# Attention and expert layer on one core: all four value products of a unit in one slot, sums and gates' products behind them

## The chip, the core and the metric

The kernel runs on one core of a Trainium2 chip. The core has TensorE (PE), VectorE (DVE), ScalarE (ACT), GpSimd (POOL) and SyncE (SP, which here only issues DMAs). The metric is the device time of one execution in microseconds, as the median of several runs. The inputs are fixed: 8 batches, 12 heads, 448 tokens, head size 64 in float32, and an expert layer over 3584 tokens with 8 experts.

## The reference, cut to what matters

```python
def rmsnorm(x, g):
    rms = np.sqrt(np.mean(x * x, axis=-1, keepdims=True) + 1e-06)
    return x / rms * g
q_n, k_n = rmsnorm(q, g_q), rmsnorm(k, g_k)
scores = np.matmul(q_n, k_n.transpose(0, 1, 3, 2)) / np.sqrt(64)
scores = scores - np.max(scores, axis=-1, keepdims=True)
attn = np.exp(scores)
attn = attn / (np.sum(attn, axis=-1, keepdims=True) + 1e-09)
x = np.matmul(attn, v)                      # -> 3584 x 768, heads next to each other
logits = x @ w_gate + modality_bias[modality_id]
# the expert with the largest logit takes the token:
#   out = probability * (relu(x @ w1[e]) @ w2[e])
```

## The kernel before, in words

The attention is cut into 48 units (`NU`) of two heads. A unit has 7 slots (`NJ`), one for each chunk of 128 of its 896 keys (the middle chunk has an end of each head). The program is written out slot by slot by the loop over `n`. What a slot does stands in a table, `plan`, which is filled from the dictionary `PLAN`: `put(slot, name, unit)`. Unit `u` has its exponentials in slots 7u to 7u+6; its other steps lie slots earlier or later. Every engine works off its own instructions strictly in the order in which they were written, so a step that waits holds all that is behind it on its engine. In one slot PE gets, in this order: the score products of the chunk (`st`), the products for the maxima of a unit two units ahead (`sa`), value products (`av`), sums (`sums`), gates' products (`gates`), transposes of keys or queries (`tr`), of the maxima (`mt`), of sums and gates (`recips`), of the output (`xt`).

The steps that the change and the prediction name, with the slot within a unit (0 to 6) before the change:

- `st`, line 849: two products (four in slot 3) into one of two PSUM banks; ACT takes the exponential out of it into `p`.
- `sa`, line 821 (816 in slot 3): one product into one of two PSUM banks (`ps_a`); DVE reduces it to the maximum of each query (`at_hlw<-sa`). The `sa` of a slot needs the bank that the reduction two slots before has read.
- `tr`, line 750: four transposes of the keys in slot 0 and of the queries in slot 3, into one of the two PSUM banks of `ps_t`, which `mt`, `recips` and `xt` share in rotation. Their operands are split into a high and a low part. ACT copies the high part (`xw<-tr`, next slot), DVE subtracts it from the value (`xw<-tr`), and DMAs that SP issues (line 763, `w1w<-xw`) move halves to the other 64 partitions. ACT makes two more copies, the last in the slot after the next. The queries' transposes are in slot 3, and the first `sa` that reads their moved half is in slot 0 of the next unit, four slots later.
- `mt`, line 832: slot 1; a transpose of the maxima, an ACT copy, and a DMA (line 837) that carries them as one more row to the score products, six slots later.
- `av`, line 888: the value products of the unit before, a pair (one for each head) for each of four chunk positions. Pairs 0, 1 and 2 are 128 rows by 64 columns, pair 3 is 64 rows by 64 columns, both heads at once in different columns of the array. Each product appears as two records of PE. Before: pairs 0 and 1 in slot 1, pair 2 in slot 4, pair 3 in slot 6. ACT copies the finished values out in the slot after pair 3 (`avcopy`).
- `sums`, line 903: every second unit, in slot 2; four products with 32 columns each that add up the exponentials over the partitions. Their operands are partial sums over the chunks (`csum`: one operation on DVE, `r2w<-r2w,half`, the others on POOL).
- `gates`, line 910: every fourth unit, in slot 6; four products with 32 columns each.
- `recips`, line 922: every fourth unit, in slot 2, three slots after the gates' products; transposes, and on DVE the reciprocals of the sums and the gate logits.
- `xt`, line 945: slot 4; four transposes of a unit's values, which DVE scales by the reciprocals (`at_w2hb<-xt,rs` or `yw<-xt,rs`); after every third unit SP issues a DMA of the rows to memory (line 961).

DVE also has the sums of squares of queries and keys (`at_hlw<-xrw`, after an ACT square), and many small operations: the inverse roots (`rstd`) and the routing (`route`, `route_pos`, `tables`). These small operations are taken from a queue by `pump`, so many a slot: nine a unit by the numbers in `pmpa` and `pmp`, most of them in slots 2 to 6. POOL multiplies the normalised queries and keys, adds partial sums, and issues the gathers and scatters.

After the attention come the experts: slots of 256 tokens with products against `w1` (line 480) and `w2` (line 510). The last units' ends are written out among the first of these.

Of the kernel before, what the change touches and what calls it, by code (L numbers as in the profile page):

```python
# [17 lines left out]
B, H, S, D = 8, 12, 448, 64  # L18
NT, DM, DFF, NE = 3584, 768, 1024, 8
CP, NCH = 112, 4  # L20
NJ = 7
NP = H // 2
NU = B * NP
# [8 lines left out]
ET = mybir.EngineType  # L32
PLAN = {'rtj': 6, 'rushat': 36, 'av': (1, 1, 4, 6), 'xt': 4, 'xte': (2, 5), 'sm': 2, 'la': 6, 'rc': 9, 'csv': (1,), 'csj': (3, 6), 'csd': (1, 1), 'cse': (2, 1), 'sa': 14, 'mt': 6, 'tk': 21, 'tq': 18, 'nq': 26, 'nk': 26, 'sk': 49, 'sq': 50, 'rs': 48, 'ld': 58, 'first': {('sq', 0): -22, ('sk', 0): -22, ('nk', 0): -21, ('nq', 0): -20, ('sq', 1): -21, ('sk', 1): -21, ('sq', 2): -20, ('sk', 2): -20, ('nk', 1): -18, ('nq', 1): -18, ('tk', 0): -18, ('tq', 0): -18, ('sa', 0): -14, ('tk', 1): -13, ('tq', 1): -11, ('sa', 1): -7, ('mt', 0): -6, ('tk', 2): -8, ('tq', 2): -8, ('nq', 2): -14, ('nk', 2): -14, ('nq', 3): -2, ('nk', 3): -1, ('sq', 3): -8, ('sk', 3): -8, ('sq', 4): -9, ('sk', 4): -9, ('sq', 6): -6, ('sk', 6): -4, ('sk', 7): -7, ('sq', 8): 5, ('sk', 8): 5, ('nk', 7): 15, ('nq', 9): 31, ('tq', 3): 4, ('mt', 1): 0, ('nq', 5): 10, ('mt', 8): 50, ('rs', 0): -21, ('rs', 2): -18, ('nq', 8): 35, ('rs', 5): -7, ('mt', 2): 8, ('nq', 7): 18, ('mt', 5): 30, ('sk', 9): 15, ('tk', 9): 43, ('mt', 6): 36, ('nq', 6): 13, ('sa', 5): 22, ('rs', 7): 0, ('rs', 8): 6, ('mt', 4): 22, ('nk', 4): 4, ('ld', 9): 6, ('tk', 5): 15}, 'rs0': {0: 0, 2: 1, 5: 0, 7: 0, 8: 2}, 'sastep': 1, 'start': -22, 'warm': {5: 2, -6: 16, -12: 4, -7: 2, -9: 4, -21: 4}, 'warmn': 2, 'early': 1, 'late0': 1, 'pmp0': 2, 'ramp': 10, 'pmp': (0, 0, 1, 1, 1, 0, 1), 'nv': [(2, 1)], 'pmpa': (1, 0, 1, 0, 1, 1, 1), 'rush': (1, 1, 1), 'ps': [(7, 1)], 'pa': [(6, 0), (6, 1), (5, 1), (5, 0)], 'rtr': 6, 'sml': 4}
MANUAL = {ET.PE, ET.DVE, ET.Activation, ET.Pool, ET.SP}
# [3 lines left out]
class Deferred:  # L38
    """Engine calls go out at once, or into the open queue."""

# [16 lines left out]
def deferred(fn):  # L57
    """What fn issues, as queue items."""
    Deferred.queue = items = []
    fn()  # L60
    Deferred.queue = None
    return items
# [3 lines left out]
def kernel(  # L66
# [25 lines left out]

    # ---------------------------------------------------------------- constants
    idn = cp.tile([128, 128], F32, name="idn")
# [83 lines left out]

    # ---------------------------------------------------------------- slot tables
    def prefix(src, nm, n):  # L180
# [19 lines left out]
    def tables(nm, ns, cnt, nb, taken, e_prev, half_blocks=None):  # L200
# [7 lines left out]
        if taken is not None:  # L208
            # blocks of at most half the size go last: columns of their own
            br = slice(NE, nv)  # L210
            nb_e = nb
            nb, cnt_e, cnt = tl("nb", [128, nv]), cnt, tl("cnt", [128, nv])
            V.scalar_tensor_tensor(out=nb[:, br], in0=nb_e, scalar=2.0, in1=half_blocks, op0=ALU.mult,
                                   op1=ALU.subtract)
            V.tensor_tensor(out=nb[:, ar], in0=nb_e, in1=nb[:, br], op=ALU.subtract)
            V.tensor_tensor(out=nb[:, ar], in0=nb[:, ar], in1=taken, op=ALU.subtract)
            for c in (ar, br):
                V.tensor_copy(out=cnt[:, c], in_=cnt_e)
# [44 lines left out]
        if taken is not None:  # L263
            # tokens of the slot
            rem = tl("rem", [128, ns], I32)
            V.tensor_tensor(out=rem, in0=cs, in1=js, op=ALU.subtract)
# [24 lines left out]
    def lists(nm, s0, ns, tb, two):  # L291
# [16 lines left out]
        def fin(a, n):  # L308
# [263 lines left out]
    def small_slot(s, xr):  # L572
        """A slot of at most 32 tokens, in a quarter of the array's columns: four column blocks at once."""
        tb, i_ = tb_of(s)
# [64 lines left out]

    # ---------------------------------------------------------------- attention  # L640
    if True:
# [100 lines left out]
        def tr(u, g):  # L742
            t, nm = T[u], "qk"[g]
            ps = ps_t.tile([128, 512], F32, tag="t", name=f"tr{u}_{g}")
            src = t["n" + nm].rearrange("p c h d -> p c (h d)")
            # keys in their own order, queries by chunk of the load
            sp = ps[:, :S].rearrange("p (t c) -> p c t", c=NCH) if g else \
# [53 lines left out]

        # Both heads' tokens on one axis, cut in chunks of 128: the middle one has an end of each.
        def columns(t, j):
            """Head and columns of the chunk's tokens."""
            if j == 3:
# [51 lines left out]
        def csum(u, h):  # L857
# [4 lines left out]
            c2 = c2_b[:, h]  # L862
            # the middle chunk's rows of this head, and the first of its chunks
            if h in CSV:
# [30 lines left out]

        # Four units at a time, each in its 32 columns of the array: the gate's products of both
        # heads in rows 0 to 15, the sums of the exponentials in rows 16 and 17.
        def sums(u):
# [151 lines left out]
        last, lastput = [-99], [-99]  # L1050
        # slots between what gives the operands and the call
        gap = {"op": 0, "act": 3, "pe": 3}
# [43 lines left out]
        for u in range(3, 6):  # L1096
            load(u)
        # engine calls of the slots to come, before and after the slot's exponential
        pre = {e: {} for e in "AV"}
# [18 lines left out]

        # what each slot does; the first units follow each other more closely
        plan = {}  # L1120

        def put(n, *what):
            plan.setdefault(n, []).append(what)
# [14 lines left out]
        for u in range(NU):  # L1138
# [4 lines left out]
            if u < NU - 1:  # L1143
                for c in range(4):
                    put(NJ * (u + 1) + (AVJ[c] if u < NU - 2 else min(AVJ[c], 6)), "av", u, c)
            put(xt_at(u), "xt", u)
            if u % 2:
                put(NJ * (u + 1) + (SMJ if u < NP * (B - 2) else P["sml"]), "sums", u - 1)
            if u % 4 == 3:
                put(NJ * (u + 2) + (LAJ if u < NP * (B - 2) else min(LAJ, 4)), "gates", u // 4)  # L1150
                put(NJ * (u + 2) + (RCJ if u < NP * (B - 2) else min(RCJ, 6)), "recips", u // 4)
            put(when("tk", u), "tr", u, 1)
# [12 lines left out]
        for n in range(P["start"], NJ * NU):  # L1165
# [100 lines left out]
            if (i + 1) % 3 == 0 and 0 < (i + 1) // 3 < 2 * B:  # L1266
                load_v((i + 1) // 3)
        # the last units' ends, among the first slot's products
        after = []

        def go(*fs):
            """Issue the calls; what a call returns (evacuations) goes out after the next one."""
            for f in fs:
# [44 lines left out]

        # the slots: the next one's operands are made among the products of this one
        small = []  # L1320
# [5 lines left out]
        for s in range(NSTAT):  # L1326
            # calls after the products of a beat
            beat = {}
# [113 lines left out]
```

## Time and profile before

| | |
|---|---|
| median of 3 runs | 1171.19 us (1169.7, 1171.19, 1174.05) |
| span of the profiled execution | 1169.2 us, 19997 instructions |
| PE / PE weight loads busy | 1105.2 us (95%) / 865.2 us (74%) |
| DVE / ACT / POOL busy | 954.4 (82%) / 815.7 (70%) / 635.6 us (54%) |
| mean granted clock of TensorE | 0.969 |
| first and last `mt` | 33.2 and 605.4 us |

The profiled execution has no other time of its own than its span. The attention's units run from about 33 to 620 us. In the views an instruction is shown by its start, its length (or, in groups, busy time and mean length), its engine, the line of the program, and output and inputs by the program's names. Most lines of DVE, ACT and POOL read L51 or L52, a helper, so these are told apart by their tiles. Matmuls are pipelined: the distance between the starts of two neighbours says more than the length of one. "<-" behind a wait names what ended it. The granted clock is a share of full speed.

### The profile page before, as it was taken

What the parts mean: (1) busy time and instruction counts of PE and PEld (TensorE: products, weight loads), DVE (VectorE), ACT (ScalarE), POOL (GpSimd) and SP (SyncE); (2) the same over time, 40 slices, a digit from 0 to 9 for tenths busy, and PEclk for the clock granted to TensorE, in tenths of its full rate; (3) what the DMA queues carried; (4) which work ended last, traced back from release to release, by engine and by line L of the source; (5) the groups of instructions that cost most, each with busy time, mean ns of one, the idle gap of its engine ahead of it and who ended that gap; (6) DMA issues with size and microseconds to landing.
All of it is one profiled execution on the core that took longest, in us unless ns stands there. A gap on an engine that the chain in (4) does not pass through costs nothing.

```text
span 1169.2 us, 19997 instructions
## 1 busy us (share of the span) xinstructions
PE 1105.2 (95%) x6678; PEld 865.2 (74%) x6678; DVE 954.4 (82%) x1812; ACT 815.7 (70%) x1569; POOL 635.6 (54%) x575
## 2 busy tenths in 40 slices
PE   8899999999989999898899999999999999999993
PEld 6555665655556555455457898999999999999991
DVE  6987889999999999899978996778677777767770
ACT  6677878777767777575566764787666877667770
POOL 3467666777567775566665456533344324454340
PEclk8899999999999999898899999999999999999997
DMA  7655557666566665454354121111153111111260
GB/s 186 148 134 144 146 152 180 166 161 153 139 141 166 164 156 142 121 138 105 102 176 157 63 42 55 52 32 54 29 217 108 42 55 42 28 55 55 69 217 17
DMA packets 101345, 131.78 MB, mean 113 GB/s; under 512 B 29979, under 2 KB 95983, under 8 KB 99696
## 3 DMA queue, kind: packets, MB, share of 16 engines
q1 hardware_dynamic: 83588, 88.57, 30.2%
q0 software_dynamic: 17616, 41.80, 11.2%
q8 instruction: 57, 0.93, 0.4%
q14 instruction: 56, 0.46, 0.2%
q10 hardware_dynamic: 28, 0.01, 0.0%
HBM read 148.74 MB, written 22.38 MB: 146 GB/s over the span
## 4 chain that ended last, share of the span: by engine, by line
PE 65%; DVE 19%; DMA 6%; ACT 4%; issue 2%; POOL 1%; SPq 1%; ACTq 0%; DVEq 0%
PE ph L480 17%; PE py L510 16%; PE st L849 10%; PE av L888 9%; DVE at_hlw L51 4%; PE sa L821 4%; DMA lt<-l_d,tb_li 3%; DVE at_hlw L52 3%; DVE w1w L51 3%; DVE xw L51 2%; PE tr L750 2%; PE px L463 2%; PE xt L945 2%; DMA w1w<-xw 1%; PE sm L903 1%
## 5 line engine op out<-in xcount | busy, mean ns | idle before, releaser
L480 PE MATMUL ph<-xw,w1w 128*128 128x256 f32 x2016 | 247.5, 284 | 3.0 <-DVE hlw L51 2.3
L480 PEld LDWEIGHTS ph<-xw,w1w 128*128 128x128 f32 x2016 | 245.3, 193 | 5.1 <-DVE hlw L51 2.5
L51 DVE TENSOR_TENSOR w1w<-r,w1w 128x256 fp32r<-128x256 f32 x360 | 220.8, 671 | 14.1 <-ACT w1w L51 14.0
L51 ACT CAST w1w<-r 128x256 fp32r<-128x256 f32 x360 | 224.9, 726 | 0.0
L51 DVE TENSOR_REDUCE at_hlw<-sa 128x1 f32<-128x448 f32 x336 | 205.3, 615 | 17.0 <-PE sa L821 11.7
L849 PE MATMUL st<-w1w 128*128 128x448 f32 (+1 forms) x480 | 193.9, 453 | 1.9 <-ACT r2w L51 1.4
L849 PEld LDWEIGHTS st<-w1w 128*128 128x128 f32 (+1 forms) x480 | 108.2, 241 | 45.9 <-ACT r2w L51 19.3
L821 PE MATMUL sa<-w1w 128*128 128x448 f32 (+1 forms) x288 | 114.9, 400 | 22.6 <-DVE at_hlw L51 22.3
L51 POOL TENSOR_TENSOR r2w<-r2w 128x448 f32<-128x448 f32 (+1 forms) x72 | 82.6, 1148 | 81.1 <-DVE r2w L51 33.6
L51 ACT ACTIVATE hhw<-ph 128x512 fp32r<-128x512 f32 x56 | 33.5, 598 | 124.5 <-PE ph L480 124.5
L51 POOL TENSOR_TENSOR xrw<-r,at_hlw 112x512 f32<-112x512 f32 x95 | 97.6, 1048 | 36.9 <-PE tr L750 11.2
L510 PE MATMUL py<-w2lw,hhw 128*128 128x384 f32 x448 | 113.8, 334 | 0.0
L51 ACT ACTIVATE r2w<-st 128x448 f32<-128x448 f32 x168 | 89.3, 541 | 33.3 <-PE st L849 30.4
L849 PE MATMUL st<-w1w,w2ha 65*128 65x448 f32 x288 | 102.4, 376 | 0.0
L51 ACT ACTIVATE at_w2lw<-st 128x448 f32<-128x448 f32 x168 | 87.9, 540 | 12.1 <-PE st L849 10.3
L51 ACT CAST w1w<-tr 64x448 fp32r<-64x448 f32 x96 | 50.5, 526 | 65.3 <-DVE xw L51 64.7
L51 POOL DMA_INDIRECT out_dram<-yw,lb_oi x22 | 26.7, 1214 | 122.2 <-ACT yw L51 112.3
L51 POOL TENSOR_TENSOR r2w<-r2w,at_w2lw 64x448 f32<-64x448 f32 (+1 forms) x48 | 54.8, 1142 | 66.7 <-DVE r2w L51 38.9
L821 PEld LDWEIGHTS sa<-w1w 128*128 128x128 f32 (+1 forms) x288 | 56.9, 198 | 35.2 <-DVE at_hlw L51 32.4
L51 DVE SCALAR_TENSOR_TENSOR hlw<-ph,hhw 128x512 fp32r<-128x512 f32 x56 | 38.7, 691 | 53.2 <-ACT hhw L51 53.2
L510 PEld LDWEIGHTS py<-w2lw,hhw 128*128 128x128 f32 x448 | 80.9, 188 | 0.0
L51 ACT ACTIVATE w1w<-tr,gs 64x448 fp32r<-64x448 f32 x96 | 60.3, 628 | 29.1 <-DVE xw L51 28.4
(296 smaller groups left out, 2414.2 us busy)
## 6 DMA issues: line engine op xcount, KB each, us to landing
w1w<-xw SPq DMA_DIRECT2D x312, 112.0 KB
r<-in_q_dram SPq DMA_DIRECT2D x48, 224.0 KB
r<-in_k_dram SPq DMA_DIRECT2D x48, 224.0 KB
w2ha<-xw SPq DMA_DIRECT2D x72, 112.0 KB
x_d<-at_w2hb SPq DMA_DIRECT2D x8, 672.0 KB
x_d<-yw SPq DMA_DIRECT2D x8, 672.0 KB
r2w<-in_v_dram SPq DMA_DIRECT2D x16, 288.0 KB
at_w2lw<-in_v_dram SPq DMA_DIRECT2D x16, 288.0 KB
```

The source lines that it names most:

```text
L51: return fn(*a, **kw)
L52: Deferred.queue.append((self.kind, lambda: fn(*a, **kw)))
L463: PE.transpose(ps[:, i, 128 * t : 128 * t + 128], xr[t][:, 2 * g + i], idn)
L480: PE.matmul(ps[:, i], lhsT=lt_, rhs=rt_[:, c], start=n == 0, stop=n == 17)
L510: PE.matmul(ps[n][:, :384], lhsT=lt_[:, j, 128 * t : 128 * t + 128], rhs=rt_[:, 384 * n : 384 * n + 384], start=j == 0 and m == 0, stop=j ...
L750: PE.transpose(sp[:, c], src[:, c], idn[:CP, :CP])
L821: PE.matmul(ps[:, :S], lhsT=t["qq"][r, h, a : a + 128], rhs=t["kk"][h][r], start=True, stop=True)
L849: PE.matmul(ps[:, :S], lhsT=l, rhs=t["qq"][:, h] if first else t["ql"][:, h], start=first and (j != 3 or h == 0), stop=not first and (j != ...
L888: PE.matmul(t["av"][64 * h : 64 * h + 64, :S], lhsT=vv[r, u % 3, j], rhs=t["p"][r, j], start=c == 0, stop=c == 3)
L903: PE.matmul(R[g][32 * i : 32 * i + 32, :S], lhsT=sel[:, m], rhs=T[u + i // 2]["cs"][:, i % 2], start=m == 0, stop=False, tile_position=(0, ...
L945: PE.transpose(ps[:CP, 128 * c : 128 * c + 128], T[u]["xt"][:, c * CP : (c + 1) * CP], idn)
```

## The change

All four value pairs of a unit go into slot 1 (`av`). The sums go behind them in slot 1, of the next unit but one instead of the next (`sm`; six slots later than before). The gates' products go behind the sums, into the same slot (`la`, from 6 to 1). The transposes of sums and gates with the reciprocals go from slot 9 (slot 2 of the next unit) to slot 4 (`rc`), and the output transposes from slot 4 to slot 0 of the same unit (`xt`), behind the keys' transposes. The special cases for the last two batches go, since the new slots need none. ACT's copy of the values follows pair 3 and so goes from slot 0 to slot 2. The number of instructions and all other slots stay as they are. The dropped lines that are only comments are left out here.

```diff
-PLAN = {'rtj': 6, 'rushat': 36, 'av': (1, 1, 4, 6), 'xt': 4, 'xte': (2, 5), 'sm': 2, 'la': 6, 'rc': 9, ...
+PLAN = {'rtj': 6, 'rushat': 36, 'av': (1, 1, 1, 1), 'xt': 0, 'xte': (2, 5), 'sm': 1, 'la': 1, 'rc': 4, ...
...
             if u < NU - 1:
                 for c in range(4):
-                    put(NJ * (u + 1) + (AVJ[c] if u < NU - 2 else min(AVJ[c], 6)), "av", u, c)
+                    put(NJ * (u + 1) + AVJ[c], "av", u, c)
             put(xt_at(u), "xt", u)
             if u % 2:
-                put(NJ * (u + 1) + (SMJ if u < NP * (B - 2) else P["sml"]), "sums", u - 1)
+                put(NJ * (u + 2) + SMJ, "sums", u - 1)
             if u % 4 == 3:
-                put(NJ * (u + 2) + (LAJ if u < NP * (B - 2) else min(LAJ, 4)), "gates", u // 4)
-                put(NJ * (u + 2) + (RCJ if u < NP * (B - 2) else min(RCJ, 6)), "recips", u // 4)
+                put(NJ * (u + 2) + LAJ, "gates", u // 4)
+                put(NJ * (u + 2) + RCJ, "recips", u // 4)
```

More of the change, by code (lines that the diff above doesn't have):

```diff
@@ L32 @@
 ET = mybir.EngineType
-PLAN = {'rtj': 6, 'rushat': 36, 'av': (1, 1, 4, 6), 'xt': 4, 'xte': (2, 5), 'sm': 2, 'la': 6, 'rc': 9, 'csv': (1,), 'csj': (3, 6), 'csd': (1, 1), 'cse': (2, 1), 'sa': 14, 'mt': 6, 'tk': 21, 'tq': 18, 'nq': 26, 'nk': 26, 'sk': 49, 'sq': 50, 'rs': 48, 'ld': 58, 'first': {('sq', 0): -22, ('sk', 0): -22, ('nk', 0): -21, ('nq', 0): -20, ('sq', 1): -21, ('sk', 1): -21, ('sq', 2): -20, ('sk', 2): -20, ('nk', 1): -18, ('nq', 1): -18, ('tk', 0): -18, ('tq', 0): -18, ('sa', 0): -14, ('tk', 1): -13, ('tq', 1): -11, ('sa', 1): -7, ('mt', 0): -6, ('tk', 2): -8, ('tq', 2): -8, ('nq', 2): -14, ('nk', 2): -14, ('nq', 3): -2, ('nk', 3): -1, ('sq', 3): -8, ('sk', 3): -8, ('sq', 4): -9, ('sk', 4): -9, ('sq', 6): -6, ('sk', 6): -4, ('sk', 7): -7, ('sq', 8): 5, ('sk', 8): 5, ('nk', 7): 15, ('nq', 9): 31, ('tq', 3): 4, ('mt', 1): 0, ('nq', 5): 10, ('mt', 8): 50, ('rs', 0): -21, ('rs', 2): -18, ('nq', 8): 35, ('rs', 5): -7, ('mt', 2): 8, ('nq', 7): 18, ('mt', 5): 30, ('sk', 9): 15, ('tk', 9): 43, ('mt', 6): 36, ('nq', 6): 13, ('sa', 5): 22, ('rs', 7): 0, ('rs', 8): 6, ('mt', 4): 22, ('nk', 4): 4, ('ld', 9): 6, ('tk', 5): 15}, 'rs0': {0: 0, 2: 1, 5: 0, 7: 0, 8: 2}, 'sastep': 1, 'start': -22, 'warm': {5: 2, -6: 16, -12: 4, -7: 2, -9: 4, -21: 4}, 'warmn': 2, 'early': 1, 'late0': 1, 'pmp0': 2, 'ramp': 10, 'pmp': (0, 0, 1, 1, 1, 0, 1), 'nv': [(2, 1)], 'pmpa': (1, 0, 1, 0, 1, 1, 1), 'rush': (1, 1, 1), 'ps': [(7, 1)], 'pa': [(6, 0), (6, 1), (5, 1), (5, 0)], 'rtr': 6, 'sml': 4}
@@ new lines @@
+PLAN = {'rtj': 6, 'rushat': 36, 'av': (1, 1, 1, 1), 'xt': 0, 'xte': (2, 5), 'sm': 1, 'la': 1, 'rc': 4, 'csv': (1,), 'csj': (3, 6), 'csd': (1, 1), 'cse': (2, 1), 'sa': 14, 'mt': 6, 'tk': 21, 'tq': 18, 'nq': 26, 'nk': 26, 'sk': 49, 'sq': 50, 'rs': 48, 'ld': 58, 'first': {('sq', 0): -22, ('sk', 0): -22, ('nk', 0): -21, ('nq', 0): -20, ('sq', 1): -21, ('sk', 1): -21, ('sq', 2): -20, ('sk', 2): -20, ('nk', 1): -18, ('nq', 1): -18, ('tk', 0): -18, ('tq', 0): -18, ('sa', 0): -14, ('tk', 1): -13, ('tq', 1): -11, ('sa', 1): -7, ('mt', 0): -6, ('tk', 2): -8, ('tq', 2): -8, ('nq', 2): -14, ('nk', 2): -14, ('nq', 3): -2, ('nk', 3): -1, ('sq', 3): -8, ('sk', 3): -8, ('sq', 4): -9, ('sk', 4): -9, ('sq', 6): -6, ('sk', 6): -4, ('sk', 7): -7, ('sq', 8): 5, ('sk', 8): 5, ('nk', 7): 15, ('nq', 9): 31, ('tq', 3): 4, ('mt', 1): 0, ('nq', 5): 10, ('mt', 8): 50, ('rs', 0): -21, ('rs', 2): -18, ('nq', 8): 35, ('rs', 5): -7, ('mt', 2): 8, ('nq', 7): 18, ('mt', 5): 30, ('sk', 9): 15, ('tk', 9): 43, ('mt', 6): 36, ('nq', 6): 13, ('sa', 5): 22, ('rs', 7): 0, ('rs', 8): 6, ('mt', 4): 22, ('nk', 4): 4, ('ld', 9): 6, ('tk', 5): 15}, 'rs0': {0: 0, 2: 1, 5: 0, 7: 0, 8: 2}, 'sastep': 1, 'start': -22, 'warm': {5: 2, -6: 16, -12: 4, -7: 2, -9: 4, -21: 4}, 'warmn': 2, 'early': 1, 'late0': 1, 'pmp0': 2, 'ramp': 10, 'pmp': (0, 0, 1, 1, 1, 0, 1), 'nv': [(2, 1)], 'pmpa': (1, 0, 1, 0, 1, 1, 1), 'rush': (1, 1, 1), 'ps': [(7, 1)], 'pa': [(6, 0), (6, 1), (5, 1), (5, 0)], 'rtr': 6}
```

## The prediction

> **What bounds the kernel now.** I read the page first (span, engines), then the busy time of the engines by stretch, then the waits of TensorE, then one unit of the attention in order of time. The span of the profiled execution is the base of the sum below; the median of the three runs, 1171.19 us, lies 2.0 us above it.
>
> ```profile
> span 1169.2 us, 19997 instructions
> ```
>
> The change acts in the attention alone, so the stretch from 60 to 600 us counts. First fence: all engines by stretch (PE, PEld, DVE, ACT, POOL busy, granted clock, DMA). Second fence: the same stretches for the value products alone (line 888).
>
> ```profile
> 60.00:240.00 180.00, 178.48 (x926) 106.94 (x924) 158.90 (x318) 144.47 (x310) 120.12 (x110) 1.00 0.61 154
> 240.00:420.00 180.00, 171.45 (x876) 101.21 (x876) 171.34 (x331) 131.44 (x287) 125.45 (x116) 0.98 0.63 151
> 420.00:600.00 180.00, 165.32 (x809) 96.69 (x805) 159.75 (x326) 113.32 (x246) 118.46 (x110) 0.93 0.54 141
> ```
>
> ```profile
> 60.00:240.00 180.00, 58.65 (x256) 14.03 (x256) 1.00 0.61 154
> 240.00:420.00 180.00, 55.49 (x238) 13.35 (x240) 0.98 0.63 151
> 420.00:600.00 180.00, 52.08 (x216) 11.90 (x212) 0.93 0.54 141
> ```
>
> A unit has eight value products, and each shows as two PE instructions, so 16 records are a unit. That gives 16.0, 14.9 and 13.5 units, or 11.25, 12.1 and 13.3 us for a unit. In the first third PE is busy 178.5 of 180 us: PE sets the pace, and DVE has 21 us to spare. In the second DVE is busy 171.3 of 180 (11.5 us a unit, 0.58 idle): DVE sets the pace. In the last third neither is full and the granted clock is 0.93. The waits of PE say the same:
>
> ```profile
> PE sa L821 <- DVE at_hlw L51: 22.3, 24, 3.0
> PE st L849 <- DMA w1w<-xw: 0.5, 1, 0.5
> ```
>
> PE waits for DVE's maxima (22.3 us in all), and practically never for the moves of the split operands through SP's queue.
>
> One unit, PE in order of time (start, length, instruction):
>
> ```profile
> 143.75 0.37 PE L821 MATMUL sa<-w1w 128*128 128x448 f32 x1
> ...
> 145.12 1.72 PE L888 MATMUL av<-r2w 128*64 128x448 f32 x8
> 146.78 0.28 PE L832 MATMUL mt<-idn,at_hlw 128*7 128x128 f32 x1
> ...
> 148.61 0.55 PE L750 MATMUL tr<-idn,xrw 112*128 112x112 f32 x4
> 148.92 0.51 PE L849 MATMUL st<-w1w 128*128 128x448 f32 x1
> ...
> 149.48 0.37 PE L821 MATMUL sa<-w1w 128*128 128x448 f32 x1
> 149.78 0.97 PE L888 MATMUL av<-r2w 128*64 128x448 f32 x4
> 150.68 0.65 PE L945 MATMUL xt<-idn,at_w2lw 128*112 128x128 f32 x4
> 151.09 0.51 PE L849 MATMUL st<-w1w 128*128 128x448 f32 x1
> ...
> 151.64 0.37 PE L821 MATMUL sa<-w1w 128*128 128x448 f32 x1
> ...
> 152.26 0.37 PE L821 MATMUL sa<-w1w 128*128 128x448 f32 x1
> 152.56 0.97 PE L888 MATMUL av<-r2w 64*64 64x448 f32 x4
> 153.46 0.56 PE L910 MATMUL sm<-at_w2hb,wg 128*32 128x448 f32 x1
> ...
> 154.34 0.54 PE L849 MATMUL st<-w1w 128*128 128x448 f32 x1
> ...
> 154.93 0.37 PE L821 MATMUL sa<-w1w 128*128 128x448 f32 x1
> ```
>
> Starts are the thing to read. A slot of scores alone, two `st` and one `sa`, takes 0.62 us (151.64 to 152.26), 0.21 a step. A pair of value products costs 0.90 us when it comes alone (149.78 to 150.68); two pairs of the same shape take 1.66 (145.12 to 146.78), so the second costs 0.76. The `sa` ahead of a value run holds PE 0.30 (149.48 to 149.78) where a plain step takes 0.21, and the score pair behind transposes takes 0.55 up to the next `sa` (151.09 to 151.64) where two plain steps take 0.41: 0.09 in, 0.14 out.
>
> **The change, part by part.** Value pairs 2 and 3 (slots 4 and 6) join pairs 0 and 1 in slot 1. Pair 2 has their shape: 0.90 becomes 0.76, and 0.09 + 0.14 of its own slot go, 0.37 in all. Pair 3 has another shape (64 rows): no row shows it behind a 128-row pair. The ends are 0.76 (same shape) and 0.90 (153.46 less 152.56); I take 0.90, since the gates' products behind it, of yet another shape, take 0.88 (to 154.34). It saves its 0.23 of entry and exit. In a sentence apart: the Trainium skill, TensorEngine Tiling (Array Packing), Key Properties, says that a change of tiling mode drains TensorE; by it pair 3 costs the 0.90, without it 0.76, and then PE would save 0.14 more a unit.
>
> The sums come six slots later, behind the values, every second unit:
>
> ```profile
> 158.87 0.57 PE L903 MATMUL sm<-at_w2hb,sel 128*32 128x448 f32 x2
> ...
> 159.76 0.65 PE L922 MATMUL sp<-idn,at_hlw 128*112 128x128 f32 x4
> ```
>
> They keep 0.89 and lose 0.23 of entry and exit: 0.12 a unit. The gates' products, every fourth unit, follow the sums in the same shape: 0.88 to 0.76, 0.03 a unit. The output transposes (0.41) move from slot 4 behind the keys' transposes in slot 0: 0.31 to 0.41, nothing taken. Sum: 0.37 + 0.23 + 0.12 + 0.03 = 0.75 us of PE a unit, 34.5 us over 46 units. That is the ceiling.
>
> Now what is late next. A unit's queries are transposed in slot 3, copied by ACT, and moved to the other partitions by SP; four slots later `sa` of slot 0 reads them.
>
> ```profile
> 161.26 0.55 PE L750 MATMUL tr<-idn,xrw 112*128 112x112 f32 x4
> 161.85 0.53 ACT L51 CAST xw<-tr 128x448 fp32r<-128x448 f32 x1
> 162.41 2.41 SPq L763 DMA_DIRECT2D w1w<-xw  x4
> ...
> 459.03 0.49 SPq L763
> 459.57 2.25 DMA w1w<-xw
> ```
>
> The last two rows are from the chain: one issue 0.49, then 2.25 to landing. Transposes to landing: 1.15 + 0.49 + 0.05 + 2.25 = 3.94 us. Today 6.32 us lie between (148.61 to 154.93), filled by pairs 2 and 3, the output transposes and the gates. After the change only scores are left: 0.31 + 0.76 + 2 x 0.62 + 0.41 = 2.73 us. PE then waits 1.21 us in front of slot 0's `sa`, and everything behind it waits: key transposes, output transposes, the value run. From that `sa` to the queries' transposes it was 4.86 us (143.75 to 148.61); with pair 2 (0.76), pair 3 (0.90) and the output transposes (0.41) it is 6.93, with sums 7.82, with gates too 8.58. Four units: 2 x 6.93 + 7.82 + 8.58 + 4 x 3.94 = 46.0 us, 11.5 each against 11.25: the first third loses 0.25 x 16 = 4.0 us. Ends for the wait: 0 (then 10.4 a unit) and 0.49 more (one other issue ahead in SP's queue).
>
> In the rest DVE decides. The long run of PE delays `sa` of slot 2, and DVE must live on its queue:
>
> ```profile
> L51 DVE TENSOR_REDUCE at_hlw<-sa 128x1 f32<-128x448 f32 x336 | 205.3, 615 | 17.0 <-PE sa L821 11.7 <-PE sa L816 4.5
> L51 DVE TENSOR_REDUCE at_hlw<-xrw 112x8 f32<-112x512 f32 x91 | 61.0, 675 | 6.9 <-ACT xrw L51 6.8
> L51 DVE SCALAR_TENSOR_TENSOR xw<-tr,gs,xw 128x448 fp32r<-128x448 f32 x48 | 32.6, 680 | 19.6 <-ACT xw L51 19.5
> L51 DVE SCALAR_TENSOR_TENSOR r2w<-r2w,half 128x448 f32<-128x448 f32 x24 | 17.7, 736 | 0.0
> L51 DVE TENSOR_TENSOR at_w2hb<-xt,rs 112x512 f32<-112x512 f32 x24 | 16.4, 683 | 5.9 <-PE xt L945 5.8
> L51 ACT ACTIVATE w1w<-tr,gs 64x448 fp32r<-64x448 f32 x96 | 60.3, 628 | 29.1 <-DVE xw L51 28.4
> ```
>
> Two `sa` banks let PE run two slots ahead. Between the maxima of slots 6 and 2 DVE has one sum over keys (0.74), two sums of squares (1.35), two maxima (1.23), the keys' subtraction (0.68) and the moved output scaling (0.68): 4.68, and three of its nine places a unit for small operations at 0.35 (11.5 less 8.4 of large ones, over nine): 5.7 us. PE needs from `sa` of slot 1 to the end of `sa` of slot 2: 0.30 + 3.32 + 0.03 + 0.56 + 0.37 = 4.58, with sums 5.47, with gates 6.2. DVE runs dry only in the last, 0.13 a unit on average. Idle today is 0.58; small operations come unevenly, so I take 0.3, which gains 0.28 a unit over 30 units: 8.4 us. Ends: nothing, and 0.45.
>
> The maxima's transpose (`mt`) follows the run and now takes the PSUM bank of the keys' transposes (two banks in rotation, output transposes between), which ACT frees only with its second copy in slot 2. DVE reaches the subtraction after about 2.7 + 0.35, then two copies of 0.63: 4.3 us against PE's 3.6, so PE waits 0.7 in units without sums. `sa` of slot 2 then ends at 5.3, inside DVE's 5.7: nothing, and 0.7 x 15 = 10 us if DVE's queue is short. ACT's copy of the values moves to slot 2 ahead of the exponential; it lies in that same wait. Reciprocals come five slots earlier; nothing waits for them before slot 0 of the next unit. SP issues the rows of x in slot 1 instead of 5, ahead of the maxima's rows, which have five slots left. POOL's queue keeps its order.
>
> Sum: 1169.2 + 4.0 - 8.4 = 1164.8, as a median 1166.8: I take 1167.
>
> **Rivals.** (B) The moves are no limit (exponentials and maxima pace slots 4 to 6 anyway, or PE is held elsewhere): then the first third gains 0.75 x 16 = 12.0 and with the 8.4 the time is 1151. For it: not one `sa` waits for such a move now. Against: nothing but 2.73 us is left between.
>
> (C) Slower, by the clock. Short stops have already halved it:
>
> ```profile
> 266.18 0.47 PE L821 MATMUL sa<-w1w 128*128 128x448 f32 x1 [1.77 <-DVE at_hlw L51]
> ...
> 265.00:270.00 5.00, 3.82 (x15) 2.51 (x15) 5.00 (x10) 1.41 (x5) 3.78 (x4) 0.78 0.27 62
> 410.00:415.00 5.00, 3.25 (x16) 2.01 (x17) 5.00 (x9) 2.56 (x8) 3.23 (x4) 1.00 0.39 88
> ```
>
> A wait of 1.77 us was followed by 0.78 in its five us; a stretch with PE busy only 3.25 of 5 kept 1.00. After the change every unit has a dense run and then a thin stretch with a 1.2 us wait in it. If the first 360 us fall to the 0.93 of the last third, that costs (0.07 + 0.05) x 180 = 22 us: 1191 less part of the 8.4 already counted, say 1187. It decides from a mean clock of about 0.97 in the first third. The Trainium skill, TensorE: Matmul & The Clock Gate, Why this matters for your kernels, sets the danger at idle gaps over about 3 us; by that this rival would not happen, and the 1.77 us row speaks against the rule.
>
> (D) The packing saves nothing: a pair costs the same wherever it stands, and all else stays: 1171. Against it the 1.66 for two pairs.
>
> **How the numbers follow.** A measurement here tells about 0.5% (6 us) from no change: faster is below 1165, slower above 1177. Forecast 0.42 (its own range 1158 to 1177; it falls below 1165 in 0.18, the same in 0.24), B 0.23, C 0.27, D 0.08 (same 0.05, slower 0.03). Faster 0.41, same 0.29, slower 0.30. The range reaches from B to C: low 1146 (B with DVE's 0.45), high 1190 (C, or 0.49 and the 10 us of `mt` on top of the forecast).
>
> **What would show it.** PE's waits: `sa` for a DMA from `xw`, near 1 us a unit in the first third (B: none). The queries' transposes to the next `sa` of slot 0: 3.9 us, not 5.5 to 6.3. Value run and pair 3 in 3.3 us; if pair 3 takes 0.76, the drain was wrong. First third: still about 16 units in 180 us (B: 17), clock 1.00 (C: below 0.97). `mt` waiting for ACT. I am wrong if the move lands sooner than 2.2 us or if DVE's small operations pile up in slots 2 to 6 while PE stands.

## The result: slower by 7%, and the profile after

| | before | after |
|---|---|---|
| median | 1172.62 us (1169.7 to 1177.33, 4 runs) | 1253.84 us (1253.11 to 1255.52, 4 runs) |
| ratio, 95% interval | | 1.0695 [1.0644, 1.0745] |
| span, mean granted clock | 1169.2 us, 0.969 | 1253.8 us, 0.936 |
| first to last `mt` | 33.2 to 605.4 us | 32.6 to 682.8 us |

The forecast was 1167, in a range up to 1190; the time lies 64 us above that end. The last row of the table places the loss: the attention's units take 650.2 us instead of 572.2, 78.0 of the 84.6 us that the span grew.

The page of the changed kernel, span and engines:

```profile
span 1253.8 us, 19942 instructions
PE 1135.7 (91%) x6678; PEld 900.7 (72%) x6678; DVE 960.1 (77%) x1812; ACT 824.4 (66%) x1569; POOL 635.5 (51%) x575
```

The work is the same (DVE 960.1 us busy against 954.4), and no engine is fuller than before. The same stretches as in the prediction, first all engines (PE, PEld, DVE, ACT, POOL busy, granted clock, DMA), then the value products alone:

```profile
60.00:240.00 180.00, 160.44 (x754) 98.23 (x754) 130.99 (x259) 118.51 (x252) 98.71 (x91) 0.90 0.50 128
240.00:420.00 180.00, 158.04 (x755) 98.14 (x755) 149.59 (x288) 117.88 (x247) 108.87 (x100) 0.90 0.56 134
420.00:600.00 180.00, 158.61 (x766) 100.52 (x764) 152.79 (x297) 117.65 (x250) 109.14 (x101) 0.91 0.53 126
```

```profile
60.00:240.00 180.00, 49.79 (x208) 14.08 (x208) 0.90 0.50 128
240.00:420.00 180.00, 46.99 (x208) 13.45 (x208) 0.90 0.56 134
420.00:600.00 180.00, 44.92 (x198) 13.17 (x200) 0.91 0.53 126
```

At 16 records a unit these are 13.0, 13.0 and 12.4 units: 13.85, 13.85 and 14.5 us each, where it was 11.25, 12.1 and 13.3. PE is busy 160.44 of 180 us where it was 178.48, DVE 130.99 where it was 158.90, and the clock went from 1.00 to 0.90. Over these stretches as a whole nobody is the bound any more; the engines wait for each other. The view of waits (us in all, times, longest) says who:

```profile
DVE at_hlw L51 <- PE sa L821: 90.8, 38, 5.6
ACT w1w L51 <- DVE xw L51: 74.6, 78, 4.8
PE sa L821 <- DVE at_hlw L51: 55.7, 52, 3.0
PE st L849 <- ACT r2w L51: 12.1, 24, 0.9
PE st L849 <- ACT at_w2lw L51: 8.8, 20, 0.9
PE mt L832 <- DVE at_w2hb L51: 0.4, 1, 0.4
PE sa L821 <- DMA w1w<-xw: 0.2, 1, 0.2
```

DVE waits for PE's maxima 90.8 us (11.7 before), and PE waits for DVE's 55.7 us (22.3 before). Both grew: that is no single bound, but two engines that take turns. The two rows of `st` are one wait, for ACT's exponentials, which go into two buffers by turns: 20.9 us (1.4 before). The last row is the one on which the forecast of the first third rested, a `sa` that waits for the move: 0.2 us in the whole run.

One unit, PE in order of time, is the piece to compare with the prediction's:

```profile
151.20 0.37 PE L821 MATMUL sa<-w1w 128*128 128x448 f32 x1
151.50 3.38 PE L888 MATMUL av<-at_w2lw,r2w 128*64 128x448 f32 x16
154.80 0.28 PE L832 MATMUL mt<-idn,at_hlw 128*7 128x128 f32 x1
...
155.38 0.37 PE L821 MATMUL sa<-w1w 128*128 128x448 f32 x1
...
156.62 0.55 PE L750 MATMUL tr<-idn,xrw 112*128 112x112 f32 x4
...
160.33 0.55 PE L849 MATMUL st<-w1w 128*128 128x448 f32 x1 [0.88 <-ACT r2w L51]
...
160.92 0.37 PE L821 MATMUL sa<-w1w 128*128 128x448 f32 x1
...
162.72 3.38 PE L888 MATMUL av<-r2w 128*64 128x448 f32 x16
166.02 0.57 PE L903 MATMUL sm<-at_hhw,sel 128*32 128x448 f32 x2
166.80 0.54 PE L910 MATMUL sm<-at_w2hb,wg 128*32 128x448 f32 x1
167.66 0.28 PE L832 MATMUL mt<-idn,at_hlw 128*7 128x128 f32 x1
```

The run of values takes 3.30 us (151.50 to 154.80); with sums and gates 4.94 (162.72 to 167.66). From the queries' transposes to `sa` of slot 0 it is 4.30 us (156.62 to 160.92), and the row that ends it is not a DMA but `st` waiting for ACT's exponential. This unit is one of the quickest; the median of that stretch is 5.25 us, with a wait for DVE's maxima in it. The same moments with all engines:

```profile
147.95 0.62 DVE L51 TENSOR_REDUCE at_hlw<-sa 128x1 f32<-128x448 f32 x1
...
153.40 0.19 DVE L52 TENSOR_TENSOR at_hlw<-at_hlw 112x48 f32<-112x48 f32 x1
...
155.79 0.62 DVE L51 TENSOR_REDUCE at_hlw<-sa 128x1 f32<-128x448 f32 x1 [2.20 <-PE sa L821]
...
157.20 0.53 ACT L51 CAST xw<-tr 128x448 fp32r<-128x448 f32 x1
157.70 0.54 ACT L51 ACTIVATE r2w<-st 128x448 f32<-128x448 f32 x1
...
157.77 0.62 DVE L51 TENSOR_TENSOR xw<-tr,xw 128x448 fp32r<-128x448 f32 x1 [0.33 <-ACT xw L51]
...
158.43 0.53 ACT L51 CAST w1w<-tr 64x448 fp32r<-64x448 f32 x1 [0.18 <-DVE xw L51]
...
158.86 0.20 ACT L51 CAST w2ha<-tr 64x64 fp32r<-64x64 f32 x1
...
159.07 0.53 ACT L51 CAST w1w<-tr 64x448 fp32r<-64x448 f32 x1
...
159.74 0.98 ACT L51 ACTIVATE r2w<-st 128x448 f32<-128x448 f32 x2
```

Two things are to be seen. DVE stood 2.20 us dry in the run of values: it had finished the maximum of slot 6 at 148.57, ahead of the run, and the last of its queue at 153.59, while the next `sa` (slot 2) came at 155.38. And after the transposes ACT has one queue: copy, exponential, four more copies, and only at 159.74 the exponentials of slots 5 and 6, for which PE's two score banks wait.

Cutting every unit at four instructions gives the ledger on which the rest of this text rests: the start of `sa` in slot 0 (ahead of the keys' transposes), the start of the value run, the start of `mt`, the start of the queries' transposes, and the next `sa` of slot 0. The means of the 35 to 38 units between 100 and 620 us of each kernel, in us:

| kernel | `sa` to run | run to `mt` | `mt` to queries | queries to next `sa` | unit |
|---|---|---|---|---|---|
| before | 1.41 | 1.65 | 2.55 | 6.80 | 12.42 |
| after | 2.54 | 4.24 | 1.85 | 5.40 | 14.03 |
| after, its floor (lowest that recurs, no sums) | 1.80 | 3.30 | 1.82 | 4.30 | 11.22 |
| e1_spread | 1.89 | 2.58 | 1.89 | 6.24 | 12.60 |
| e2_values | 1.58 | 3.57 | 2.40 | 5.54 | 13.09 |
| e4_extra_products | 1.87 | 4.02 | 1.86 | 6.04 | 13.78 |
| e5_small_ops_in_run | 2.09 | 4.05 | 1.82 | 4.90 | 12.87 |
| e8_small_ops_and_products | 1.89 | 3.98 | 1.84 | 5.63 | 13.34 |
| e10_pair2_joined | 1.46 | 2.45 | 2.46 | 6.33 | 12.71 |
| e13_copy_on_dve | 2.30 | 4.14 | 1.82 | 5.05 | 13.32 |

I call the fourth stretch the thin one: after the change PE has only scores there. The three in front of it grew by 3.02 us (5.61 to 8.63); the thin one gave back 1.40.

The waits can be laid on the same stretches, here for 34 of the units after the change and 37 before. After the change PE stands, in gaps of over 0.1 us, for 0.03 us a unit in the three front stretches together, and for 1.58 in the thin one: 1.21 for DVE's maxima, 0.35 for ACT's exponentials (before: 0.46 in the thin one, all for DVE). DVE is busy 95% of the thin stretch, and only 70 and 60% of the two ahead of it. So PE sets the pace of the front, DVE that of the thin stretch. The front is longer than its quickest units for another reason, the clock. The first stretch of two neighbouring units, the unit above and the next:

```profile
148.63:151.50 2.87, 2.87 (x14) 2.35 (x12) 2.87 (x6) 1.93 (x5) 2.00 (x2) 0.59 0.41 135
160.92:162.72 1.80, 1.80 (x14) 1.43 (x12) 1.22 (x2) 1.80 (x4) 1.72 (x2) 1.00 0.82 219
```

PE is busy all the time in both, with 14 records each: 2.87 us at a clock of 0.59, 1.80 at 1.00. Over all these units the granted clock after the change is 0.68, 0.94, 1.00 and 0.95 in the four stretches (before: 0.98, 1.00, 0.99 and 0.95).

### The profile page after: what moved, and what is told of

It reads as the page before. It is cut to its first block, busy times and chain, and to the rows that moved or that the text cites. A ratio compares the mean times of both kernels' runs of the same rounds, so it can differ in the third digit from the quotient of the medians.

```text
span 1253.8 us, 19942 instructions
## 1 busy us (share of the span) xinstructions
PE 1135.7 (91%) x6678; PEld 900.7 (72%) x6678; DVE 960.1 (77%) x1812; ACT 824.4 (66%) x1569; POOL 635.5 (51%) x575
## 4 chain that ended last, share of the span: by engine, by line
PE 61%; DVE 18%; DMA 8%; ACT 6%; issue 4%; POOL 1%; SPq 1%; ACTq 0%; DVEq 0%; POOLq 0%
PE ph L480 16%; PE py L510 15%; PE av L888 11%; PE st L849 8%; DVE at_hlw L51 4%; DVE at_hlw L52 4%; DMA lt<-l_d,tb_li 3%; DMA w1w<-xw 3%; PE sa L821 3%; DVE xw L51 2%; PE tr L750 2%; DVE w1w L51 2%; PE xt L945 2%; PE sm L903 2%; ACT w1w L51 2%
## 5 line engine op out<-in xcount | busy, mean ns | idle before, releaser
L51 DVE TENSOR_REDUCE at_hlw<-sa 128x1 f32<-128x448 f32 x336 | 204.7, 616 | 97.7 <-PE sa L821 90.8
L849 PE MATMUL st<-w1w 128*128 128x448 f32 (+1 forms) x480 | 199.8, 467 | 22.4 <-ACT r2w L51 12.1
L821 PE MATMUL sa<-w1w 128*128 128x448 f32 (+1 forms) x288 | 125.2, 435 | 56.0 <-DVE at_hlw L51 55.7
L849 PEld LDWEIGHTS st<-w1w 128*128 128x128 f32 (+1 forms) x480 | 111.6, 246 | 46.4 <-ACT r2w L51 24.7
L821 PEld LDWEIGHTS sa<-w1w 128*128 128x128 f32 (+1 forms) x288 | 61.0, 212 | 80.7 <-DVE at_hlw L51 76.9
L849 PE MATMUL st<-w1w,w2ha 65*128 65x448 f32 x288 | 106.0, 388 | 0.0
```

What stands on the lines that cost most here:

```text
L51: return fn(*a, **kw)
L821: PE.matmul(ps[:, :S], lhsT=t["qq"][r, h, a : a + 128], rhs=t["kk"][h][r], start=True, stop=True)
L849: PE.matmul(ps[:, :S], lhsT=l, rhs=t["qq"][:, h] if first else t["ql"][:, h], start=first and (j != 3 or h == 0), stop=not first and (j != ...
```

## The experiments

Theory A: the work moved into the run lengthens the front by its full price, while the thin stretch is held by ACT's and DVE's queues and can't shrink by as much; and because PE is held there, DVE has caught up when the run begins and stands dry in it. The rivals were that one part of the change alone is at fault, that DVE's subtraction holding ACT is, or that the clock is.

### Which part: one alone, the others alone, one pair

Two of the rows that the theories below use: e1_spread and e2_values, the waits of DVE for PE and of PE for DVE.

```profile
DVE at_hlw L51 <- PE sa L821: 35.0, 36, 3.6
PE sa L821 <- DVE at_hlw L51: 27.0, 32, 3.2
```

```profile
DVE at_hlw L51 <- PE sa L821: 46.3, 38, 3.4
PE sa L821 <- DVE at_hlw L51: 38.5, 43, 2.7
```

e1_spread, the changed kernel with the value pairs back in their slots:

```diff
-'av': (1, 1, 1, 1)
+'av': (1, 1, 4, 6)
```

> The changed kernel with the value pairs back in slots 1, 1, 4, 6; sums, gates' products, reciprocals and output transposes stay where the change put them. Theory A (the one long value run is what costs: DVE runs dry in it, and the thin slots behind it are paced by ACT and DVE): 1160 to 1180 us, DVE's idle time in front of its maxima back near 17 us, clock near 0.97. Theory B (the other moves cost: output transposes in slot 0, the maxima's transpose waiting for their bank, sums six slots later): over 1220 us.

Measured: 1191.65 us, 1.0124 [1.0078, 1.0171], above the range of theory A; DVE's wait for the maxima is 35.0 us, not near 17.

e2_values, the kernel before with only the value pairs moved:

```diff
-'av': (1, 1, 4, 6)
+'av': (1, 1, 1, 1)
...
-at(pre["A"] if j else post, n + (j > 0), lambda u=u: avcopy(u))
+at(pre["A"], n + 6, lambda u=u: avcopy(u))
```

> The kernel before with all four value pairs in slot 1 and nothing else moved (ACT's copy of the values held in slot 0 of the next unit, where it was). Theory A: 1220 to 1260 us, a unit of 13 us or more from the first third on. Theory B: 1160 to 1180 us.

Measured: 1206.05 us, 1.0245 [1.0206, 1.0284], between the two ranges: neither theory had it.

The values alone cost 31 us (1206.05 less 1174.9) and all else alone 17; both together cost 81 (1253.84 less 1172.62). No part alone is at fault, and 33 us come only from the two together. (ACT's copy of the values in slot 2 is in neither of the two runs; what it costs is in the 33 and was not tried by itself.) In e2 the run grew by 1.92 us a unit and the thin stretch shrank by 1.26.

e10_pair2_joined and e11_pair3_to_pair2, the kernel before with one pair moved:

```diff
-'av': (1, 1, 4, 6)
+'av': (1, 1, 1, 6)     # e10: pair 2 joins 0 and 1
+'av': (1, 1, 4, 4)     # e11: pair 3 joins pair 2 in slot 4
```

> The kernel before with value pair 2 alone joined to pairs 0 and 1 (slots 1, 1, 1, 6). By the shape saving alone (0.37 us of TensorE a unit in the first third): 1163 to 1170. Theory A: DVE's cover in slot 1 holds for a run of 2.4 us, but the stretch behind loses 1.1 us of TensorE's work and falls to the 4.3 us that ACT and DVE need there at least, so little or nothing is gained: 1168 to 1182. If every value pair moved ahead costs in proportion (a third to a half of the 31 us of all): 1182 to 1190.

> The kernel before with value pair 3 moved from slot 6 to slot 4, behind pair 2 (slots 1, 1, 4, 4): one entry and exit less (0.23 us of TensorE a unit), no longer run in slot 1, and as much work of TensorE between the queries' transposes and the next unit's first maxima product but for that 0.23. Theory A: 1160 to 1173. If any longer run costs: 1176 to 1190.

Measured: e10 1187.41 us, 1.0099 [1.0069, 1.0129]; e11 1177.85 us, 1.002 [0.9998, 1.0043]. In e10 the run grew by 0.80 us where 0.76 was costed, and the thin stretch fell by 0.47: the packing saves PE time as reckoned, and the kernel still loses. Theory A expected 1168 to 1182; the time lies where a cost in proportion to the pairs moved was expected, so theory A set the loss too low. Joining two pairs within the thin stretch (e11) brings nothing that can be measured; theory A's 1160 to 1173 was missed.

### What holds the thin stretch

e6_queries_earlier, the changed kernel with the queries' transposes one slot earlier:

```diff
-'tq': 18
+'tq': 19
```

> The changed kernel with the queries transposed one slot earlier (slot 2), so that copies, subtraction and move have five slots. If the way of the queries (copies on ACT, DMA to landing) is what the first maxima product waits for: 20 to 45 us less, 1210 to 1235. If it is the load of DVE and ACT in the thin slots: 1245 to 1260.

Measured: 1235.75 us, 1.0544 [1.0504, 1.0583]: 18 us of the 81 come back. The time lies 0.75 us above the first range and far below the second, so both causes may have a part.

e13_copy_on_dve and e14_before_copy_on_dve give the second pair of copies of the queries' transposes to DVE, in the changed kernel with the small operations of e5 (below), and in the kernel before:

```diff
-A.copy(t["qq"][HI, 1], ps[HI, :S])
-A.copy(qm_b[u % 2][HI, 64:128], ps[HI, 0:64])
+E_ = V.tensor_copy if u >= 2 else A.copy
+E_(t["qq"][HI, 1], ps[HI, :S])
+E_(qm_b[u % 2][HI, 64:128], ps[HI, 0:64])
...
-at(pre["A"], n + 2, a2)
+at(pre["A"] if a[1] or a[0] < 2 else pre["V"], n + 2, a2)
```

> The changed kernel with the small operations issued in the value run (as in e5), and besides the second pair of copies of the queries' transposes (128x448 halves, 0.53 and 0.20 us on ACT) given to DVE. Theory A (ACT's one queue of two pairs of copies and the exponentials sets the floor of the stretch from the queries' transposes to the next unit's first sa, 4.30 us in its best units) expects that floor to fall by up to 0.7 us and the median of the stretch below 4.3, and the time 5 to 30 us under e5's 1210: 1180 to 1205. The rival (ACT's queue is no limit there; DVE's maxima or the bank of scores pace it) expects the floor to stay at 4.3 and the time to rise by what DVE takes over, 1208 to 1235.

> The kernel before with the same copies given to DVE, nothing else. There the stretch holds value products and is 5.4 to 6.3 us long for TensorE's own work, so theory A expects no gain from a lighter ACT and a loss from DVE's 0.7 us more a unit where DVE sets the pace: 1175 to 1205. The rival (ACT's queue delays the kernel before as well) expects a gain: 1145 to 1168.

Measured: e13 1225.43 us, 1.0416 [1.036, 1.0473] (e5: 1.0339); e14 1198.18 us, 1.0164 [1.0121, 1.0207]. The floor of the thin stretch did fall, from 4.30 to 3.95 us, as theory A expected, so ACT's queue did set it. PE's waits for ACT's exponentials show the same: 32.5 us in e5, 2.0 in e13. But the time did not fall: it lies in the rival's range, 0.8% above e5, which is at the edge of the two intervals. In e13's best units the next limit shows at once (all engines, one unit):

```profile
189.91 0.63 DVE L51 CAST w1w<-tr 64x448 fp32r<-64x448 f32 x1 [0.17 <-ACT xw L51]
...
190.46 0.22 DVE L51 CAST xw<-tr 64x64 fp32r<-64x64 f32 x1
...
190.71 1.16 DVE L51 TENSOR_REDUCE at_hlw<-sa 128x1 f32<-128x448 f32 x2
...
191.39 0.47 PE L822 MATMUL sa<-w1w 128*128 128x448 f32 x1 [0.28 <-DVE at_hlw L51]
```

The `sa` now waits for DVE's maximum, behind the copy that DVE took over. So ACT sets the floor in e5, DVE follows close behind it, and to relieve the one by loading the other gains nothing (PE's waits for DVE rise from 24.9 to 47.7 us). In the kernel before, the same edit only costs.

### DVE's small operations

e5_small_ops_in_run issues DVE's small operations beside the run of values instead of in the thin stretch; e7_before_small_ops makes the same edit in the kernel before; e9_ops_and_queries is e5 with e6.

```diff
-'pmp': (0, 0, 1, 1, 1, 0, 1) ... 'pmpa': (1, 0, 1, 0, 1, 1, 1)
+'pmp': (0, 4, 0, 0, 0, 0, 1) ... 'pmpa': (1, 0, 3, 0, 0, 0, 0)
```

> The changed kernel with the same nine places a unit for DVE's small operations (units 0 to 35), seven of them in slots 1 and 2, so that DVE does them during the value run, instead of six in slots 2 to 6 behind it. Theory A (DVE dry in the run, then too much of DVE in the thin slots): DVE's idle time in front of its maxima falls from 90.8 us below 60, the stretch from the queries' transposes to the next first maxima product falls from 5.25 (median) to 4.3 to 4.7 us, and the time to 1210 to 1235. If ACT's queue or the move of the split queries sets that stretch: no shorter than 5 us, time unchanged within 10 us.

> The kernel before with the places for DVE's small operations of the kernel that has seven of them in slots 1 and 2; its values stay in slots 1, 1, 4, 6. Theory A: no gain, since DVE isn't dry there: 1172 to 1195. If that placing is simply better: under 1168.

> The changed kernel with both: small operations in slots 1 and 2, and the queries transposed in slot 2. If the load of DVE and the queue of ACT behind the queries' copies are two parts of one stretch: 1185 to 1205, clock over 0.96, still slower than the kernel before, since the front (first maxima product to queries' transposes) keeps its 2.6 us more. If the two work on the same wait: 1205 to 1215, as with the small operations alone.

Measured: e5 1210.08 us, 1.0339 [1.0287, 1.0391]; e7 1193.14 us, 1.0117 [1.0031, 1.0203]; e9 1198.16 us, 1.022 [1.0169, 1.027]. e5, the first third by engine, and the two waits:

```profile
60.00:240.00 180.00, 161.94 (x824) 100.10 (x822) 139.60 (x292) 129.15 (x278) 111.48 (x101) 0.97 0.55 140
```

```profile
DVE at_hlw L51 <- PE sa L821: 55.7, 41, 5.0
PE sa L821 <- DVE at_hlw L51: 24.9, 18, 3.9
```

This is the largest piece: 44 of the 81 us, with no operation taken away. DVE's dry time falls from 90.8 to 55.7 us and PE's waits from 55.7 to 24.9, the thin stretch comes to its floor of 4.30 in the median unit, and the clock of the first third is back at 0.97. The operations also become shorter: those of line 52 take DVE 141.67 us for 261 between 100 and 600 us after the change, 0.54 each, and 115.96 us for 326 in e5, 0.36 each. What of the 44 us is the place and what the shorter operations is not separated here. In the kernel before the same edit loses (there the run is 1.65 us, too short, I take it, for four of them). So a good part of the loss hangs on where the small operations stand, beside the run or behind it. e9 lies in the range of two parts of one stretch: both edits help. What PE still waits for in e9 is ACT's exponentials, 36.5 us (1.4 before), and DVE's maxima, 25.0 (22.3 before).

### ACT held by DVE's subtraction

e3_sub_later emits DVE's subtraction on the split of the queries one slot later in the changed kernel; e12_before_sub_later does so for queries and keys in the kernel before.

```diff
-at(pre["V"], n + 1, d_)
+at(pre["V"], n + (2 if a[1] == 0 and a[0] >= 6 else 1), d_)     # e3
+at(pre["V"], n + (2 if a[0] >= 6 else 1), d_)                   # e12
```

> The changed kernel with DVE's subtraction for the queries one slot later, behind ACT's copies out of the same bank instead of between them. If ACT, held between its copies until DVE has subtracted, keeps the exponentials of slots 5 and 6 and so the scores of slot 0: the stretch from the queries' transposes to the next unit's first maxima product falls from a median near 5.25 to about 4.2 us, and the time by up to 1.0 x 46 = 46 us, to 1210 to 1235. If the move of the split queries sets that stretch (3.94 us by the recorded prediction): no shorter than 4.2 and the time unchanged within 10 us.

> The kernel before, with DVE's subtraction on the split of the queries and the keys emitted one slot later in the units from the seventh on, so that it stands less often in the middle of ACT's chain of copies. In the kernel before ACT waits 93.0 us for that subtraction. Theory A (TensorE and DVE set the pace of the kernel before by turns, and ACT's waits lie beside them) expects the wait to shrink and the time to stay within 1 per cent, 1165 to 1183 us. The rival (ACT's held chain delays the next unit's first sa in every unit, so that the stretch from the queries' transposes to it shortens) expects at least 0.3 us a unit, 1150 to 1163 us.

Measured: e3 1251.24 us, 1.0649 [1.0604, 1.0695]; e12 1175.62 us, 1.0014 [0.9991, 1.0036]. ACT's wait in e3, then in e12:

```profile
ACT w1w L51 <- DVE xw L51: 35.1, 30, 2.4
```

```profile
ACT w1w L51 <- DVE xw L51: 12.9, 8, 5.0
```

The wait fell from 74.6 to 35.1 us after the change and from 93.0 to 12.9 before it, and the time stayed within 3 us both times. In e3 the lowest thin stretch did fall, from 4.30 to 4.03 us, one more sign that ACT's queue sets that floor; but the median only went from 5.25 to 5.17, since PE's wait for DVE's maxima stayed (61.7 us, 55.7 without the edit). A large wait in the view can be worth nothing, where it lies beside other work.

### The clock

e4_extra_products adds nine products a unit to the thin stretch of the changed kernel, written to a score bank ahead of the scores, which overwrite them. e8_small_ops_and_products is e4 with e5.

```diff
+if j in (5, 6, 0) and 2 < u < NU - 3:
+    for _ in range(3):
+        PE.matmul(ps[:, :128], lhsT=ones, rhs=idn, start=True, stop=True)
```

> The changed kernel with three more products of 128 columns (their result is overwritten) ahead of the scores of slots 5, 6 and 0 of nearly every unit, to keep TensorE busy in the thin stretch. If the dropped clock (0.90 from 60 to 600 us) is a cause of its own: clock 0.97 or more and 1215 to 1240 us. If the waits are the cause and the low clock only follows from them: clock up, and the time unchanged within 10 us or longer by up to the 0.2 x 9 x 43 = 77 us that the added products take.

> The changed kernel with the small operations in slots 1 and 2 and the three extra products ahead of the scores of slots 5, 6 and 0. If waits and low clock are two costs: clock over 0.965 and 10 to 20 us less than with the small operations alone. If the extra products now lie on the way: 5 to 40 us more than with the small operations alone.

Measured: e4 1244.85 us, 1.0588 [1.0562, 1.0614]; e8 1220.7 us, 1.0405 [1.0362, 1.0449]. e4, the first third:

```profile
60.00:240.00 180.00, 171.83 (x974) 118.25 (x973) 132.47 (x263) 120.81 (x255) 100.22 (x92) 0.96 0.50 128
```

With the clock back at 0.96, the first stretch falls from 2.54 to 1.87 us and the run from 4.24 to 4.02, 0.89 us a unit together, or 41 us over 46 units: an estimate of what the low clock, and what comes with it, takes in these stretches. But the products themselves lengthen the thin stretch by 0.64 us, 29 us, so some 12 should be left; 9 were measured by the medians, 12.5 by the ratios. By the recorded ranges that is the second case, a time unchanged within 10 us or so, and not the 1215 to 1240 of a clock that is a cause of its own. Where e5 has already lifted the clock of the first third to 0.97 the same products cost 11 us, as the second case of e8 expected. The clock is a real part of the loss, but it follows from PE's waits in the thin stretch; what takes those away mends it too.

None of these kernels beats the kernel before. How e9's remaining 23 us (1198.16 less 1174.67) divide between the longer front, ACT's queue and the clock stays open.

## Why the prediction was wrong, point by point

- **PE's prices: right to a hundredth.** Pair 3 behind pair 2 costs the 0.90 (the run of four pairs 3.30, that of three in e10 at least 2.40), the run 3.30 (costed 3.32), with sums 4.19. The floor of the first three stretches is 1.80 + 3.30 + 1.82 = 6.92 us, predicted 6.93; with the sums 7.81 against 7.82. Rival D (the packing saves nothing) is wrong: the saving is there.
- **The move as the limit of the thin stretch: wrong limiter.** Predicted 3.94 us for the DMA; no `sa` waited for it beyond 0.2 us. The floor is 4.30, by ACT's queue, and e13 and e3 show it: with copies off ACT 3.95, with ACT not held by the subtraction 4.03. The step "only scores are left: 2.73" counted PE's work and the move, but not ACT's two pairs of copies and the exponentials that stand in one queue behind the same transposes. Term: 3.94 costed, 5.40 measured on average, 1.46 a unit. Of these, 0.36 are ACT's floor; the other 1.10 are mostly the next step's fault, DVE's maxima, for which PE waits 1.21 us a unit there.
- **"DVE must live on its queue" of 5.7 us: the step that failed worst.** It took PE to run two slots ahead of DVE when the run begins. That was so before, when PE set the pace; after, PE is held in the thin stretch, and DVE has caught up. In the unit shown above PE takes the time that was costed from `sa` of slot 1 to the end of `sa` of slot 2 (151.20 to 155.79, 4.59 us; costed 4.58), but DVE has only 2.39 us of its queue left (to 153.59), and is dry for the other 2.20. What it does not do there it does in the thin stretch, where PE then waits for it. DVE is dry 90.8 us in all, 2.0 a unit over 46 units, where 0.13 to 0.3 was taken; PE's waits for DVE went from 22.3 to 55.7 us, and the gain of 8.4 us became a loss. The warning at the prediction's end, small operations that pile up in slots 2 to 6 while PE stands, is what happened; placed in the run instead, they give back 44 us (e5).
- **The clock (rival C): its condition was met.** It was to decide from 0.97 in the first third; measured 0.90. But its price of 22 us was worked out on the old lengths, and its 1187 left the other two losses out. They come together: the waits of the thin stretch lower the clock, and the low clock falls on the products behind them. The first stretch is where that shows, 2.54 us against 1.80, at a mean clock of 0.68.
- **Rival B (the move is hidden anyway, 1151): its reason was right, its time wrong.** The move is no limit; what holds PE is ACT and DVE.
- **`mt` waiting for the bank of the keys' transposes: did not happen.** PE's `mt` waited 0.4 us in all. The output transposes cost 0.42 (floor of the first stretch 1.80, less the 1.38 of before's median unit), costed 0.41.
- **The sum.** Predicted 11.5 us a unit, 7.57 in front and 3.94 thin; measured 14.03, 8.63 and 5.40. The front is 1.06 over its price, by the clock (PE waits there for 0.03 us a unit); the thin stretch is 1.46 over, by ACT's floor and DVE's maxima. By thirds, against the forecast's own units: (13.85 - 11.5) x 16.0 = 37.6; (13.85 - 11.82) x 14.9 = 30.2; (14.5 - 13.02) x 13.5 = 20.0. That is 87.8 of the 89.0 us between the forecast's 1164.8 and the span of 1253.8.

## What to carry to other kernels

Packing work into one place on a busy engine saves only if every engine that lives off it has as much to do, at that moment, as the packed run lasts, and if the place that it leaves is not held by someone else. Work out the emptied stretch for each queue, not for the engine that gains and the one transfer that is in sight: here the stretch that ACT's queue sets was 0.36 us longer than the 3.94 costed for the DMA, and DVE's, on average, longer than both. And an engine's backlog read before a change is no property of the kernel; it vanishes when the engine ahead of it is slowed. Of the edits tried here, moving the starved neighbour's small work beside the run gave back most (44 of 81 us); in the kernel before, where the run is short, the same edit lost.

## What the runs showed of the hardware

The clock can drop at waits well under two microseconds. The changed kernel around one `sa` of slot 6, PE, DVE and POOL in order of time, and then two stretches of 5 us with the columns of the stretches above (the granted clock is the third number from the end):

```profile
143.10 0.18 DVE L52 TENSOR_SCALAR at_hlw<-at_hlw 112x48 int32<-112x48 int32 x1
...
144.06 1.15 POOL L51 TENSOR_TENSOR r2w<-r2w,at_w2lw 64x448 f32<-64x448 f32 x1 [3.13 <-PE tr L750]
144.12 1.13 DVE L52 TENSOR_SCALAR at_hlw<-at_hlw 112x48 int32<-112x48 int32 x1
...
147.08 0.47 PE L821 MATMUL sa<-w1w 128*128 128x448 f32 x1 [1.27 <-DVE at_hlw L51]
...
149.01 0.95 PE L750 MATMUL tr<-idn,xrw 112*128 112x112 f32 x4
```

```profile
140.00:145.00 5.00, 5.00 (x31) 3.29 (x27) 3.11 (x5) 2.91 (x6) 1.87 (x2) 1.00 0.21 47
145.00:150.00 5.00, 3.55 (x14) 2.67 (x13) 4.97 (x13) 3.95 (x10) 1.92 (x3) 0.76 0.71 182
```

After a wait of 1.27 us for DVE the keys' transposes take 0.95 us instead of 0.55, and the clock of these five us is 0.76. The clock records of this trace hold only 1.00 and 0.50: here 0.50 from 147.59 to 151.00, 3.41 us. All low times between 60 and 620 us last 3.41 us or two or three times that, and begin whole multiples of 3.41 us apart, so where a wait falls between these marks may matter as much as its length. No threshold comes out of these traces: waits of 1.12 us in one thin stretch (from 293.31) were followed by a low clock, waits of 1.60 (from 393.27) were not, and neither were the 1.75 us at 412.32 in the kernel before. The Trainium skill, TensorE: Matmul & The Clock Gate, Why this matters for your kernels, asks only for no idle gaps over about 3 us; this measurement differs, and decides here.

DVE's small operations are dearer than the 0.35 us that I took: in the kernel before those of line 52 take 165.10 us for 314 between 100 and 600 us, 0.53 each. The same rows show one reason. An operation of the same kind and shape takes 0.18 us while POOL stands, and 1.13 us when it starts inside an operation of POOL, ending 0.04 us after it (144.12 + 1.13 against 144.06 + 1.15). Three more of DVE's small operations in these two units, at 139.83, 145.71 and 149.79, end 0.04 to 0.06 us after the operation of POOL that they started in. The Trainium skill, SBUF — State Buffer, SBUF: two separate sides, says that DVE, in some kinds of operation, and GpSimd share a pair of ports which the one that starts first holds for its whole instruction while the other is blocked; the trace agrees for this operation.
